# Both heads of a pair in one two-bank score tile, one low-rank add, key copies on ScalarE

## The chip, the cores and the metric

The kernel runs on 1 core of one Trainium2 chip. The metric is device time in microseconds (us) of one execution. A core has TensorE (PE; its weight loads are shown apart as PEld), VectorE (DVE), ScalarE (ACT), GpSimd (POOL) and SyncE (SP), which here only issues DMAs. TensorE writes its results to PSUM, eight banks of 512 float32 columns on 128 partitions.

## What is computed

Two stages. The first is attention in which a query sees the first 8 positions and its own last 96, with a bias that grows with distance; the second is a mixer: a low-rank sum over positions, then a two-layer network, each with a residual.

```python
# q, k, v: (4, 8, 768, 64); n_global 8, n_local 96
scores = q @ k.T / 8
dist   = n_local where is_global & ~is_local, else |i - j|
scores = scores - slope[h] * dist          # slope[h] = 2**-(h + 1) for 8 heads
scores = where(is_global | is_local, scores, -1e9)
a      = softmax(scores)                   # over the keys
x      = (a @ v) with the heads side by side: (4, 768, 512)

h   = x.T @ U @ V                          # U: (768, 32), V: (32, 768)
u   = x + h.T
out = u + relu(u @ w_ch1) @ w_ch2          # w_ch1: (512, 2048), w_ch2: (2048, 512)
```

## The kernel before

The order of instructions on every engine is written out by hand; a framework adds the semaphores. Work goes in pairs of heads: 4 batches of 4 pairs, index `i` from 0 to 15, batch `i // 4`. One pass of the main loop (L774) works on pair `i` and finishes pair `i - 1`.

**Attention of a pair.** The stages are small functions. `cast_qk` turns loaded queries and keys to fp16; `st_T` (pairs 1 to 7) turns them over on TensorE, `turn` (pairs 8 to 15) by DMA. `st_K` (L332) makes `kA`, the keys with the first 8 columns of every block but the first replaced by the global keys, by two VectorE copies. `scores(i, c)` computes chunk `c` of three (512, 512 and 384 columns of a band of 1408) for both heads. The two heads lie in the two halves of the 128 partitions, so their matmuls (L360, L367) have 64 rows each. Each head's scores go to a PSUM tile of one bank, tag `sc`, two buffers.

For batch 0, before the main loop, the bias is added by TensorE (L352) and `st_SE` takes the exponents from PSUM, head by head (L379). Chunks with odd `i + c` use the two `cps` banks instead of `sc`. For the other batches `st_S` lets VectorE add the bias: `s_dve` (L392) computes `score * scale / slope[h] + relcat` into an SBUF tile `sp{hi}`, one step per head and chunk, and `st_E` takes one exponent per head over 1408 columns, scaled by the head's slope (L404). `st_V` multiplies by the values into the bank `ob`, divides (L425, L439), and GpSimd casts the result to `x16` (L440).

**The low-rank sum.** `st_M1` multiplies `x16` by U; for batches 1 to 3 `st_MT` turns the result over with one matmul (L466), of which VectorE copies input and output (`zw` L453, `tmp` L467). `st_M3` multiplies by V in two calls of three matmuls (L503), the first into `sc`, the second into `ob`, one unit of the network later; each call adds its half to `x_sb` (L508). The second also has GpSimd cast `x_sb` to `x16` (L512), and `st_X` issues the DMA that turns that over into `uT`. Batch 0 goes another way (`st_M2`): sums in PSUM, copies to `uT` (L485, L487).

**The network.** Its work is cut into units of about 0.87 us of TensorE, which `fill(n)` puts between the attention steps: *up* units (eight matmuls L609 into a bank of a ring of three, then a relu on ScalarE into `htr`, L614) and *down* units. The first downs are four matmuls of 512 columns (L639). For the last five of the twelve groups of 256 positions (`WG`, L68) the down product is a 2x2 block product with seven instead of eight multiplications: `mk_product` (L659) makes x1, y1, y2, x2, y3, x3, x4, in the last group x1, y1, x2, y2, x3, y3, x4, each followed by an add to `x_sb` (L664). They need sums of the halves of `htr`, s1 to s4, in two parts of 0 to 3 and 4 to 7 of their eight blocks, and sums of weights in `t16`. These VectorE sums are queued as jobs (`queue_sum`); `fill` issues one after each unit, and `need` issues those that a product is about to read. After the main loop the remaining units run alone.

**Around the first main pass.** The bias steps of pair 4, chunk 0, stand by hand between other steps (L763 to L769):

```python
    s_dve(NP, 0, first[0])
    begin_up(0, (0, 1), ps_cps("hps"))
    st_M1(NP - 1)
    s_dve(NP, 1, first[1])
    begin_up(0, (2,))
    begin_up(1, (0, 1, 2), ps_th("hps"))
    st_M2(NP - 1)
```

Of the kernel before, what the change touches and what calls it, by code (L numbers as in the profile page):

```python
# [20 lines left out]
def kernel(  # L21
# [13 lines left out]
    nc = tc.nc  # L35
# [43 lines left out]

    def ps_sc(tag="sc"):  # L80
        return psum.tile([P, 512], FP32, name="sc", tag=tag, bufs=2)

# [82 lines left out]
    warm(8)  # L165
    setup = scp.tile([P, 384], I32, name="setup", tag="ep0")
    reli = setup[:, 0:256]
# [14 lines left out]
    nc.vector.tensor_copy(ident16, ident)  # L182
    relcat = cst.tile([P, 640], FP32, name="relcat")
    rel16 = cst.tile([P, 3, 256], BF16, name="rel16")
# [16 lines left out]
    for vt in vbuf:  # L201
        nc.gpsimd.memset(vt[:, :, :, D:D + 1], 1.0)
    nc.gpsimd.tensor_copy(relcat[:, 0:512].rearrange("p (a c) -> p a c", a=2), rel3[:, 0:2])
    nc.gpsimd.tensor_copy(relcat[:, 512:640], relB[:, 0:P])
    finish_table(
        relcat, relcat[0:NG, 0:512].rearrange("p (a c) -> p a c", a=2)[:, :, P:]
    )

# [134 lines left out]
    def scores(i, c, on_pe):  # L343

        kT, kA, qT = kts[i], kas[i], qts[i]
        c0 = 512 * c
        tot = min(512, W - c0)
        r0 = 256 if c else 0
        scs = [ps_sc("cps" if on_pe and (i + c) % 2 else "sc") for hi in range(2)]
        if on_pe:  # L350
            for hi in range(2):
                nc.tensor.matmul(  # L352
                    scs[hi][:, 0:tot], slI[:, 2 * (i % NP) + hi],
                    rel16.rearrange("p a c -> p (a c)")[:, r0:r0 + tot], start=True, stop=False,
                )
        for kb in (2 * c, 2 * c + 1):
            o = 256 * kb - c0
            for hi in range(2):
                r = slice(hi * D, (hi + 1) * D)
                nc.tensor.matmul(  # L360
                    scs[hi][:, o:o + P], kT[r, kb * P:(kb + 1) * P], qT[r, kb * P:(kb + 1) * P],
                    start=(o == 0 and not on_pe), stop=(o + P == tot),
                )
            if kb < NSB - 1:
                for hi in range(2):
                    r = slice(hi * D, (hi + 1) * D)
                    nc.tensor.matmul(  # L367
                        scs[hi][:, o + P:o + 2 * P], kA[r, kb], qT[r, (kb + 1) * P:(kb + 2) * P],
                        start=False, stop=(o + 2 * P == tot),
                    )  # L370
        return [(sc, c0, tot, r0) for sc in scs]

    def st_SE(i, c):

        if c == 0:
            for hi in range(2):
                eps[i, hi] = scp.tile([P, W], FP16, name=f"ep{hi}", tag=f"ep{hi}")
        for hi, (sc, c0, tot, _) in enumerate(scores(i, c, True)):
# [4 lines left out]
    relfs = (relcat[:, 0:512], relcat[:, 256:512].unsqueeze(1).broadcast_to((P, 2, 256)), relcat[:, 256:640])  # L383

    def s_dve(i, hi, got):
        sc, c0, tot, r0 = got
        if c0 == 0:
            sps[i, hi] = scp.tile([P, W], FP32, name=f"sp{hi}", tag=f"sp{hi}", bufs=1)
        dst, got = sps[i, hi][:, c0:c0 + tot], sc[:, 0:tot]
        if c0 == 512:  # L390
            dst, got = (t.rearrange("p (a c) -> p a c", a=2) for t in (dst, got))
        nc.vector.scalar_tensor_tensor(  # L392
            out=dst, in0=got,
            scalar=qk_scale / slope[2 * (i % NP) + hi], in1=relfs[c0 // 512],
            op0=ALU.mult, op1=ALU.add,
        )

    def st_S(i, c):
        for hi, got in enumerate(scores(i, c, False)):
            s_dve(i, hi, got)  # L400

    def st_E(i, hi):
        ep = scp.tile([P, W], FP16, name=f"ep{hi}", tag=f"ep{hi}")
        nc.scalar.activation(  # L404
            ep, sps.pop((i, hi)), AF.Exp, scale=slope[2 * (i % NP) + hi]
        )
        eps[i, hi] = ep

    def st_V(i, hi):
        b, h = i // NP, 2 * (i % NP) + hi  # L410
        ep, vt, vA = eps.pop((i, hi)), vts[i], vas[i]
        obf = ps_cps("ob") if (i, hi) == (NP - 1, 1) else ps_ob()
# [13 lines left out]
        xo = xs[b][:, :, h * D:(h + 1) * D]  # L426
        x16 = x16s[b][:, i % NP, :, hi * D:(hi + 1) * D]
        rb = rcp.unsqueeze(2).broadcast_to((P, NSB, D))
# [14 lines left out]
    def st_M1(i):  # L443
        b, dc = i // NP, i % NP
        ch = slice(dc * P, (dc + 1) * P)
        if b:
            tps = ps_ob()
            for n in range(NSB):
                nc.tensor.matmul(
                    tps[:, 0:R], x16s[b][:, dc, n], u16[:, n, 0:R],  # L450
                    start=(n == 0), stop=(n == NSB - 1),
                )
            nc.vector.tensor_copy(turn16[i % 2][:, 0:R], tps[:, 0:R])  # L453
            return
        tps = ps_th("tmp_ps")
        for n in range(NSB):
            nc.tensor.matmul(
                tps[:, 0:P], u16[:, n], x16s[b][:, dc, n],
                start=(n == 0), stop=(n == NSB - 1),
            )  # L460
# [8 lines left out]
    def st_M2(i):  # L469
        b, dc = i // NP, i % NP  # L470
        ch = slice(dc * P, (dc + 1) * P)
        for g in range(2):
# [5 lines left out]
            for t in range(NTG):  # L478
                nc.tensor.matmul(
                    ups[:, t * P:(t + 1) * P], x16s[b][:, dc, NTG * g + t], ident16,  # L480
                    start=False, stop=(t == NTG - 1),
                )
# [7 lines left out]
    def st_X(i):  # L490
        b, dc = i // NP, i % NP
        nc.sync.dma_start_transpose(
            uTs[b][:, dc].rearrange("d (n p) -> d n p", n=NSB),
            x16s[b][:, dc].rearrange("p n d -> p (n d)"),
        )

    def st_M3(i, g):
# [13 lines left out]
        if g == 1:  # L511
            nc.gpsimd.tensor_copy(x16s[b][:, dc], xs[b][:, :, ch])  # L512

# [21 lines left out]
    jobs = deque()  # L535
    have = set()

    def queue_sum(name, part, out_, a, b_, op):
        def go():
            nc.vector.tensor_tensor(out_, a, b_, op)  # L540
# [33 lines left out]
    def queue_group(b, g):  # L574
# [9 lines left out]
        def queue_sums(k):  # L584

            h = cell["htr"]
            if k == 0:
                for x in range(1, 5):
                    cell[f"s{x}"] = ffp.tile([P, HJ, P], FP16, name=f"s{x}", tag=f"s{x}", bufs=1)
                cell.update(a11=h[:, 0:HJ, 0:P], a12=h[:, HJ:NJC, 0:P],  # L590
                            a21=h[:, 0:HJ, P:FT], a22=h[:, HJ:NJC, P:FT])
# [99 lines left out]
    def fill(n):  # L691
        for _ in range(n):
            unit()
            if jobs:
                jobs.popleft()()

# [21 lines left out]
    for i in range(NP):  # L718
# [33 lines left out]
        if i == 2:  # L752
            load_w1(1)
        st_SE(i, 2)
        if i >= 2:
# [18 lines left out]
    for i in range(NP, NPAIR + 2):  # L774
# [116 lines left out]
```

## Time and profile before

| | |
|---|---|
| median of 3 runs | 233.54 us (232.63 to 234.28) |
| the profiled execution | 232.94 us |
| its span, first to last instruction | 231.0 us |
| TensorE busy | 223.2 us (97%), 2324 matmuls |
| VectorE busy | 152.7 us (66%), 350 instructions |
| ScalarE busy | 110.9 us (48%), 167 instructions |
| GpSimd busy | 80.5 us (35%), 131 instructions |
| granted TensorE clock, mean | 1.000 |

The profile is one execution. A group of instructions is told by its source line, engine, operation and tile, as output<-input, with the shape as partitions x elements and its count; then follow the busy time, the mean of one in ns, and how long the engine had idled before it and for whom. In a timeline a row gives start, duration, engine, line and operation; a bracket at its end tells an idle time before it and what ended that. Matmuls are pipelined: their starts are measured, their ends are modelled.

### The profile page before, as it was taken

The numbers are of one execution on the slowest core, as the hardware profiler recorded it, in microseconds if no ns is written. First come the engines' busy times: TensorE is split into PE (matmuls) and PEld (weight loads), VectorE is DVE, ScalarE is ACT, GpSimd is POOL, SyncE is SP. The second block draws the span as 40 slices with busy tenths as digits, with TensorE's granted clock in tenths as the row PEclk, the third lists the DMA queues.
The fourth block names the chain that finished last, engine by engine and source line by source line (L and its number), as shares of the span: only waits on it lengthen the run. The fifth ranks groups of instructions, "written<-read, shape, count | busy, mean of one in ns | idle before, by whom it ended". The sixth has DMA issues, their size and how long they took to land.

```text
span 231.0 us, 5678 instructions
## 1 busy us (share of the span) xinstructions
PE 223.2 (97%) x2324; PEld 161.8 (70%) x2324; DVE 152.7 (66%) x350; ACT 110.9 (48%) x167; POOL 80.5 (35%) x131
## 2 busy tenths in 40 slices
PE   7989999999999999999999999999999999999994
PEld 2455678788644457766666656866688888888883
DVE  3697797868677667566656675779895524444452
ACT  6776957685621313827363707473633334333320
POOL 6399728577444243433424051504120100000000
PEclk9999999999999999999999999999999999999999
DMA  6997998999999999897786955633131302011112
GB/s 183 321 280 201 280 203 188 261 259 175 213 210 244 209 315 216 220 182 188 157 226 134 258 140 145 148 100 79 32 81 48 79 3 91 1 48 45 45 48 91
DMA packets 86561, 36.66 MB, mean 159 GB/s; under 512 B 74152, under 2 KB 83592, under 8 KB 86536
## 3 DMA queue, kind: packets, MB, share of 16 engines
q1 hardware_dynamic: 81480, 32.01, 55.1%
q0 software_dynamic: 5056, 4.29, 12.3%
q8 instruction: 18, 0.29, 0.5%
q14 instruction: 7, 0.06, 0.1%
HBM read 27.46 MB, written 6.29 MB: 146 GB/s over the span
## 4 chain that ended last, share of the span: by engine, by line
PE 86%; POOL 3%; DMA 3%; ACT 3%; DVE 2%; issue 1%; SPq 1%; POOLq 0%
PE hps L609 35%; PE cps L639 22%; PE cx L659 8%; PE cy L659 5%; PE sc L360 4%; DMA vst<-in_v_dram 3%; PE ob L420 2%; PE ob L416 2%; PE sc L367 2%; ACT htr L614 1%; ACT ep L404 1%; PE tp L250 1%; PE sc L503 1%; PE ob L503 1%; SPq L105 1%
## 5 line engine op out<-in xcount | busy, mean ns | idle before, releaser
L614 ACT ACTIVATE htr<-hps 128x512 f16<-128x512 f32 x96 | 56.6, 598 | 85.0 <-PE hps L609 82.2
L609 PE MATMUL hps<-uT,w 128*128 128x256 f16 x756 | 96.2, 273 | 0.5 <-DVE uT L485 0.3
L609 PEld LDWEIGHTS <-w 128*128 128x128 f16 x756 | 70.5, 98 | 11.3 <-issue 0.4
L639 PE MATMUL cps<-w,htr 128*128 128x512 f16 x224 | 56.9, 379 | 0.0
L392 DVE SCALAR_TENSOR_TENSOR sp<-sc,relcat 128x512 f32<-128x512 f32 (+1 forms) x72 | 43.3, 641 | 15.5 <-PE sc L360 8.9
L404 ACT ACTIVATE ep<-sp 128x1408 f16<-128x1408 f32 x24 | 32.8, 1374 | 16.3 <-DVE sp L392 16.3
L512 POOL CAST x<-x_sb 128x768 f16<-128x768 f32 x12 | 10.3, 856 | 60.5 <-DVE x_sb L508 60.5
L639 PEld LDWEIGHTS <-htr 128*128 128x128 f16 x224 | 19.1, 97 | 16.6
L440 POOL CAST x<-x_sb 128x384 f16<-128x384 f32 x30 | 15.8, 525 | 26.8 <-DVE x_sb L439 26.7
L360 PEld LDWEIGHTS <-kT 64*128 64x128 f16 x192 | 8.2, 93 | 15.1 <-issue 13.5
L540 DVE TENSOR_TENSOR s<-htr 128x512 f16<-128x512 f16 x20 | 9.3, 464 | 12.7 <-ACT htr L614 12.7
L439 DVE TENSOR_TENSOR x_sb<-ob,rcp 128x384 f32<-128x384 f32 x30 | 16.7, 558 | 1.0
L659 PEld LDWEIGHTS <-s 128*128 128x128 f16 x160 | 15.5, 98 | 1.8
L360 PE MATMUL sc<-qT,kT 64*128 64x128 f16 x192 | 16.7, 221 | 0.0
L420 PE MATMUL ob<-v,ep 128*128 128x65 f16 x192 | 16.2, 193 | 0.0
L420 PEld LDWEIGHTS <-ep 128*128 128x128 f16 x192 | 13.8, 98 | 2.7 <-ACT ep L379 0.3
L664 DVE TENSOR_TENSOR x_sb<-cx,x_sb 128x256 f32<-128x256 f32 x20 | 8.5, 423 | 10.1 <-PE cx L659 10.0
L136 POOL CAST v<-vst 128x768 f16<-128x768 f32 x16 | 13.4, 839 | 4.5 <-DMA vst<-in_v_dram 4.5
L367 PE MATMUL sc<-qT,kA 64*128 64x128 f16 x160 | 14.1, 216 | 0.9 <-DVE kA L286 0.9
L379 ACT ACTIVATE ep<-sc 128x512 f16<-128x512 f32 (+1 forms) x24 | 12.0, 559 | 5.1 <-PE sc L367 4.8
L416 PE MATMUL ob<-vA,ep 128*128 128x65 f16 x160 | 14.3, 194 | 0.2 <-DVE vA L312 0.2
L659 PEld LDWEIGHTS <-htr 128*128 128x128 f16 x120 | 11.7, 98 | 1.3
(102 smaller groups left out, 269.4 us busy)
## 6 DMA issues: line engine op xcount, KB each, us to landing
qst<-in_q_dram SPq DMA_DIRECT2D x16, 384.0 KB, 4.2
kst<-in_k_dram SPq DMA_DIRECT2D x16, 384.0 KB, 4.9
vst<-in_v_dram SPq DMA_DIRECT2D x16, 384.0 KB, 3.4
out_dram<-x_sb SPq DMA_DIRECT2D x23, 256.0 KB, 2.3
w<-in_moe_w_ch_dram POOLq DMA_DIRECT2D x8, 512.0 KB, 8.9
vA<-v SPq DMA_DIRECT2D x8, 152.3 KB, 4.3
out_dram<-x_sb SPq DMA_DIRECT2D x2, 128.0 KB, 1.7
uT<-x SPq DMA_TRANSPOSE x12, 2.8
```

What stands on the lines that cost most here:

```text
L360: nc.tensor.matmul(scs[hi][:, o:o + P], kT[r, kb * P:(kb + 1) * P], qT[r, kb * P:(kb + 1) * P], start=(o == 0 and not on_pe), stop=(o + P ...
L367: nc.tensor.matmul(scs[hi][:, o + P:o + 2 * P], kA[r, kb], qT[r, (kb + 1) * P:(kb + 2) * P], start=False, stop=(o + 2 * P == tot),)
L392: nc.vector.scalar_tensor_tensor(out=dst, in0=got, scalar=qk_scale / slope[2 * (i % NP) + hi], in1=relfs[c0 // 512], op0=ALU.mult, op1=ALU ...
L404: nc.scalar.activation(ep, sps.pop((i, hi)), AF.Exp, scale=slope[2 * (i % NP) + hi])
L416: nc.tensor.matmul(ob[:, qi], ep[:, OF[qi - 1]:OF[qi - 1] + P], vA[:, qi - 1, hi], start=True, stop=False,)
L420: nc.tensor.matmul(ob[:, qi], ep[:, DG[qi]:DG[qi] + P], vt[:, qi, hi], start=(qi == 0), stop=True,)
L439: nc.vector.tensor_tensor(xo, ob[:, :, 0:D], rb, ALU.mult)
L440: nc.gpsimd.tensor_copy(x16, xo)
L609: nc.tensor.matmul(hps[:, k * FT:(k + 1) * FT], w1_16[:, dc, jt * P:(jt + 1) * P], uT[:, dc, ts], start=(dc == 0 and k == 0), stop=(dc == ...
L614: nc.scalar.activation(cell["htr"][:, 2 * jp:2 * jp + 2].rearrange("p j t -> p (j t)"), hps, AF.Relu)
L639: nc.tensor.matmul(cps, htr[:, jc, t * P:(t + 1) * P], w2_16[:, jc], start=(b > 0 and jc == 0), stop=(jc == NJC - 1),)
L659: nc.tensor.matmul(ps, cell[a][:, j], tw[w][:, j], start=(first and j == 0), stop=(done is not None and j == HJ - 1), skip_group_check=True,)
```

## The change

- `ps_sc` gives one tile of two banks, one buffer. `scores` puts head 0 in its first bank and head 1 in its second; where the `cps` banks are used, nothing is changed.
- The bias table has a second half, the first times 0.5 (`st_R`, one multiplication, issued in the third round of batch 0). The slope of head 1 is half that of head 0, so one step with head 0's slope serves both heads: `s_dve` handles both, `sp` and `ep` hold both, and `st_E` scales both exponents by head 0's slope. In batch 0 one exponent step takes both heads of a chunk that lies in `sc`.
- `st_M3` is one call with six matmuls into the two-bank tile and one add of 768 columns; the cast to `x16` follows at the place of the former first call. `st_X` stays where it was.
- `x16` is a tile per pair, three buffers, instead of one per batch, two buffers.
- `st_K` copies the keys on ScalarE, without the 8 global columns; VectorE fills those for all five blocks.
- s3 is written over a quarter of `htr`; `t16` has a buffer of its own instead of one of `x_sb`. Jobs for s1 to s4 may be issued by `fill` only two units later than before.

```diff
-    def ps_sc(tag="sc"):
-        return psum.tile([P, 512], FP32, name="sc", tag=tag, bufs=2)
+    def ps_sc():
+        return psum.tile([P, 2, 512], FP32, name="sc", tag="sc", bufs=1)
...
-        x16s[b] = xp.tile([P, NP, NSB, P], FP16, name="x16", tag="x16")
...
-        nc.vector.tensor_copy(kA.rearrange("d n p -> d (n p)"), kT[:, 0:S - P])
+        nc.scalar.copy(kA[:, :, NG:], kT.rearrange("d (n p) -> d n p", n=NSB)[:, 0:NSB - 1, NG:])
         nc.vector.tensor_copy(
-            kA[:, 1:, 0:NG], kT[:, 0:NG].unsqueeze(1).broadcast_to((P, NSB - 2, NG))
+            kA[:, :, 0:NG], kT[:, 0:NG].unsqueeze(1).broadcast_to((P, NSB - 1, NG))
         )
...
-        scs = [ps_sc("cps" if on_pe and (i + c) % 2 else "sc") for hi in range(2)]
+        both = None if on_pe and (i + c) % 2 else ps_sc()
+        scs = [ps_cps("sc") if both is None else both[:, hi] for hi in range(2)]
...
+        if both is not None:
             nc.scalar.activation(
-                eps[i, hi][:, c0:c0 + tot], sc[:, 0:tot], AF.Exp, scale=qk_scale
+                eps[i][:, :, c0:c0 + tot], both[:, :, 0:tot], AF.Exp, scale=qk_scale
             )
...
+    def st_R():
+        nc.vector.tensor_scalar_mul(relcat2[:, 1], relcat, 0.5)
+
+    relfs = (relcat2[:, :, 0:512], relcat2[:, :, 256:768], relcat2[:, :, 256:640])
...
         nc.vector.scalar_tensor_tensor(
-            out=dst, in0=got,
-            scalar=qk_scale / slope[2 * (i % NP) + hi], in1=relfs[c0 // 512],
+            out=sps[i][:, :, c0:c0 + tot], in0=both[:, :, 0:tot],
+            scalar=qk_scale / slope[2 * (i % NP)], in1=relfs[c0 // 512],
             op0=ALU.mult, op1=ALU.add,
         )
...
-            ep, sps.pop((i, hi)), AF.Exp, scale=slope[2 * (i % NP) + hi]
-        )
+            eps[i][:, hi], sps[i][:, hi], AF.Exp, scale=slope[2 * (i % NP)]
+        )
...
-        ups = ps_ob() if g else ps_sc()
-        for t in range(NTG):
-            n = NTG * g + t
+        ups = ps_sc()
+        for n in range(NSB):
+            g, t = divmod(n, NTG)
             nc.tensor.matmul(
-                ups[:, t * P:(t + 1) * P], v16w[:, n * P:(n + 1) * P], tmps[b][:, ch],
+                ups[:, g, t * P:(t + 1) * P], v16w[:, n * P:(n + 1) * P], tmps[b][:, ch],
                 start=(t == 0), stop=(t == NTG - 1),
             )
-        dst = xs[b][:, NTG * g:NTG * (g + 1), ch]
+        dst = xs[b][:, :, ch].rearrange("p (g t) d -> p g t d", g=2)
         nc.vector.tensor_tensor(
-            dst, ups[:, 0:GT].rearrange("p (t d) -> p t d", t=NTG), dst, ALU.add
-        )
-        if g == 1:
-            nc.gpsimd.tensor_copy(x16s[b][:, dc], xs[b][:, :, ch])
+            dst, ups[:, :, 0:GT].rearrange("p g (t d) -> p g t d", t=NTG), dst, ALU.add
+        )
+        nc.gpsimd.tensor_copy(x16s[i], xs[b][:, :, ch])
...
-    def queue_sum(name, part, out_, a, b_, op):
+    count = [0]
+
+    def queue_sum(name, part, out_, a, b_, op, wait=0):
         def go():
             nc.vector.tensor_tensor(out_, a, b_, op)
             have.add((name, part))
-        jobs.append(go)
+        jobs.append((count[0] + wait, go))
...
-        t = xp.tile([P, 3, HJ, HD], FP16, name="t16", tag="x_sb", bufs=3)
+        t = wbig.tile([P, 3, HJ, HD], FP16, name="t16")
...
-                queue_sum((name, b, g), k, cell[name][:, js], cell[a][:, js], cell[b_][:, js], op)
+                queue_sum((name, b, g), k, cell[name][:, js], cell[a][:, js], cell[b_][:, js], op, wait=2)
...
             unit()
-            if jobs:
-                jobs.popleft()()
+            count[0] += 1
+            if jobs and jobs[0][0] < count[0]:
+                jobs.popleft()[1]()
...
         if i == 2:
             load_w1(1)
+            st_R()
         st_SE(i, 2)
...
     st_M2(NP - 2)
-    s_dve(NP, 0, first[0])
+    s_dve(NP, first)
     begin_up(0, (0, 1), ps_cps("hps"))
     st_M1(NP - 1)
-    s_dve(NP, 1, first[1])
     begin_up(0, (2,))
...
         if i > NP:
-            st_M3(i - 1, 0)
+            st_M3(i - 1)
         if live:
             st_E(i, 1)
         fill(next(units))
         if i > NP:
-            st_M3(i - 1, 1)
             st_X(i - 1)
```

More of the change, by code (lines that the diff above doesn't have):

```diff
@@ L165 @@
     warm(8)
-    setup = scp.tile([P, 384], I32, name="setup", tag="ep0")
+    setup = scp.tile([P, 384], I32, name="setup", tag="ep")
     reli = setup[:, 0:256]
@@ L182 @@
     nc.vector.tensor_copy(ident16, ident)
-    relcat = cst.tile([P, 640], FP32, name="relcat")
+    relcat2 = cst.tile([P, 2, 768], FP32, name="relcat")
+    relcat = relcat2[:, 0]
     rel16 = cst.tile([P, 3, 256], BF16, name="rel16")
@@ L202 @@
         nc.gpsimd.memset(vt[:, :, :, D:D + 1], 1.0)
[L203 to L206, printed above, removed]
-    )
+    relcat3 = relcat.rearrange("p (a c) -> p a c", a=3)
+    nc.gpsimd.tensor_copy(relcat3, rel3)
+    finish_table(relcat, relcat3[0:NG, :, P:])
     def load_uv():
@@ L370, in scores, with s_dve @@
                     )
[L371 removed]
+        return scs, both, c0, tot
     def st_SE(i, c):
         if c == 0:
[L376 to L378 removed]
+            eps[i] = scp.tile([P, 2, W], FP16, name="ep", tag="ep")
+        scs, both, c0, tot = scores(i, c, True)
+        if both is not None:
             nc.scalar.activation(
[L380 removed]
+                eps[i][:, :, c0:c0 + tot], both[:, :, 0:tot], AF.Exp, scale=qk_scale
             )
[L383 to L386 removed]
+            return
+        for hi, sc in enumerate(scs):
+            nc.scalar.activation(
+                eps[i][:, hi, c0:c0 + tot], sc[:, 0:tot], AF.Exp, scale=qk_scale
+            )
+    def st_R():
+        nc.vector.tensor_scalar_mul(relcat2[:, 1], relcat, 0.5)
+    relfs = (relcat2[:, :, 0:512], relcat2[:, :, 256:768], relcat2[:, :, 256:640])
+    def s_dve(i, got):
+        _, both, c0, tot = got
         if c0 == 0:
[L388 to L391, printed above, removed]
+            sps[i] = scp.tile([P, 2, W], FP32, name="sp", tag="sp", bufs=1)
         nc.vector.scalar_tensor_tensor(
[L393 to L394 removed]
+            out=sps[i][:, :, c0:c0 + tot], in0=both[:, :, 0:tot],
+            scalar=qk_scale / slope[2 * (i % NP)], in1=relfs[c0 // 512],
             op0=ALU.mult, op1=ALU.add,
@@ L398, in st_S @@
     def st_S(i, c):
-        for hi, got in enumerate(scores(i, c, False)):
-            s_dve(i, hi, got)
+        s_dve(i, scores(i, c, False))
     def st_E(i, hi):
-        ep = scp.tile([P, W], FP16, name=f"ep{hi}", tag=f"ep{hi}")
+        if hi == 0:
+            eps[i] = scp.tile([P, 2, W], FP16, name="ep", tag="ep")
         nc.scalar.activation(
-            ep, sps.pop((i, hi)), AF.Exp, scale=slope[2 * (i % NP) + hi]
+            eps[i][:, hi], sps[i][:, hi], AF.Exp, scale=slope[2 * (i % NP)]
         )
-        eps[i, hi] = ep
     def st_V(i, hi):
         b, h = i // NP, 2 * (i % NP) + hi
-        ep, vt, vA = eps.pop((i, hi)), vts[i], vas[i]
+        ep, vt, vA = eps[i][:, hi], vts[i], vas[i]
+        if hi == 0:
+            x16s[i] = xp.tile([P, NSB, P], FP16, name="x16", tag="x16", bufs=3)
         obf = ps_cps("ob") if (i, hi) == (NP - 1, 1) else ps_ob()
```

18 lines of the change are left out of this document (9 added, 9 removed).

## The prediction

> **What bounds the kernel.** I read the page's busy times first, then busy time by stage, then the groups by shape, and last the timelines of four places. The profiled execution took 232.94 us; its span is 231.0, so 1.94 lie around it, which the change does not touch. The median of the runs is 233.54, 0.60 above the profiled one.
>
> Busy time by stage (us of PE, PEld, DVE, ACT, POOL in each stretch; the columns after them are clock, DMA share, GB/s):
>
> ```profile
> 0.00:35.00 35.00, 30.86 (x381) 19.36 (x382) 25.82 (x67) 24.29 (x48) 23.57 (x48) 1.00 0.99 246
> 35.00:180.00 145.00, 144.64 (x1511) 99.94 (x1509) 104.80 (x227) 70.83 (x94) 56.12 (x83) 1.00 0.79 175
> 180.00:231.00 51.00, 47.68 (x437) 42.48 (x435) 22.11 (x57) 15.82 (x27) 0.83 (x1) 1.00 0.15 51
> ```
>
> From 35 to 180 us TensorE is busy for 144.64 of 145.00, at granted clock 1.00, and VectorE has 40 us to spare. The change keeps every matmul (2324 before and after), so nothing it saves on VectorE or ScalarE there can shorten the run by more than the few waits of TensorE. Measured as starts that come later than the column counts of the matmuls explain, the waits of over 70 ns after 34 us, row-group switches left out, are six: 0.25, 0.16, 0.21, 0.08, 0.17 and 0.39, together 1.26 us. What the change can add, it adds where TensorE is waiting on others or would soon be: the first 35 us and the last 10.
>
> **The parts.** The prices come from these groups (busy us, mean ns | idle before):
>
> ```profile
> L392 DVE SCALAR_TENSOR_TENSOR sp<-sc,relcat 128x512 f32<-128x512 f32 x48 | 31.0, 685 | 6.6 <-PE sc L367 5.7 <-ACT ep L404 0.4
> L392 DVE SCALAR_TENSOR_TENSOR sp<-sc,relcat 128x384 f32<-128x384 f32 x24 | 12.3, 552 | 8.9 <-PE sc L360 8.9
> L272 ACT COPY qT<-tp 128x768 f16<-128x768 f16 x7 | 5.6, 804 | 0.3 <-PE tp L250 0.2
> L122 DVE CAST k<-kst 128x768 f16<-128x768 f32 x2 | 1.1, 546 | 0.0
> ```
>
> *Bias step.* 685 and 552 ns give 1.04 ns a column and 152 ns fixed, so one step over 2x512 is 1.22 us and over 2x384 0.95. Back to back, two old steps took 1.28 and 1.02: VectorE gains about 0.06 x 36, 2 us in all, where it has 40 spare. New wait: one step must wait for both exponents of the pair before, which read the same tile. Head 1's exponent ended after head 0's step had started three times (41.20, 51.18 and 61.30 against 40.12, 50.71 and 60.83), so the merged step ends about 0.5 later there. Behind it are the reciprocal, the division and the key turn on VectorE; TensorE comes back for the score tile at 43.20, 53.32 and 62.96, 0.4 to 0.9 after the new ends (42.45, 52.44, 62.55). Price 0. If that cover is gone, up to 0.5 each.
>
> *The first merged step* is different: it used to be split around a small copy.
>
> ```profile
> 29.85 0.68 DVE L392 SCALAR_TENSOR_TENSOR sp<-sc,relcat 128x512 f32<-128x512 f32 x1
> 30.45 0.28 DVE L461 CAST tmp<-tmp_ps 128x128 f16<-128x128 f32 x1
> ...
> 31.01 0.33 PE L474 MATMUL ups<-v16w,tmp 128*128 128x384 f16 x1
> ```
>
> The copy moves from 30.45 to 29.85 + 1.14 = 30.99 and ends at 31.27; the matmul that reads it starts at 31.01 now and at 31.30 then, and TensorE already waits at 32.15 for what follows it. **+0.3**, between 0.2 and 0.5.
>
> *Half-slope table.* One new 128x768 f32 multiplication on VectorE at about 22.2 us, ahead of the uT copies. Between 20.4 and 27.1 VectorE idles 0.14 us before 23.27 and little else, and at 27.13 TensorE waits for its last copy, so nearly all of it shows. Alone it is near the L122 cast, 0.55 (a 1x rate, as 953 ns in L273, would make it 0.95). But GpSimd is casting then, and a VectorE copy that meets GpSimd can be held:
>
> ```profile
> 22.01 0.89 POOL L122 CAST q<-qst 128x768 f16<-128x768 f32 x1
> 22.85 0.82 POOL L122 CAST k<-kst 128x768 f16<-128x768 f32 x1
> ...
> 37.61 2.40 DVE L312 COPY vA<-v 8x520 f16<-8x520 f16 x1 [0.47 <-POOL vA L299]
> ```
>
> The 8x520 copy takes 0.27 alone; here it sat until GpSimd's two casts ended at 39.86. In six other meetings (0.46 to 0.84 us) it got in after one GpSimd instruction. Three values: held by nothing, VectorE is 0.31 late at 23.27 and 0.2 at 27.13; held by the q cast to 22.90, the multiplication ends near 23.4, the k cast after it near 24.2 (TensorE's k transposes need it at 23.73), and 27.13 becomes 27.9, **+0.8**; held by both casts to 23.67, VectorE runs 1.85 late at 23.27 and 27.13 becomes 28.5, +1.4. I take 0.8, the commoner row.
> The Trainium skill (SBUF — State Buffer, Who interferes with whom) says that VectorE's two-port modes and GpSimd share one port pair, that whoever issues first holds it for the whole instruction and the other blocks fully; the 2.40 us row agrees. By that rule alone the multiplication waits for the q cast only, and the sum is the middle one.
>
> *Exponents of batch 0.* Six pairs become one step of 2x512 or 2x384: 595 and 488 ns give 0.84 a column, so 1.02 against 1.09 for a pair. The score tile of chunk (2,0) is freed at 15.87 instead of 15.36 and its matmul waits 0.17, but that chunk waits at 16.71 for key copies anyway. 0.
>
> *Key copies.* VectorE loses 319 ns, ScalarE gains 600 columns (from 475 ns at 384 and 804 at 768, about 0.66) eight times. ScalarE idles over half the span; behind the copy stand a relu and an exponent, and three hps banks cover about 3 us. The keys are used 2.5 us later or more. 0; if the banks ran out, up to 0.66 each.
> The Trainium skill (ScalarE: Activation LUTs, Rules for kernel authors) puts simple elementwise work on VectorE, not ScalarE; 319 ns against an estimated 660 agrees. By it the move loses 0.34 x 8 = 2.7 us of engine time, none of it on the path.
>
> *Low-rank sum, x16, t16.* Two adds of 556 ns become one of about 0.95; six matmuls stand together and need both score banks, free since the third bias step, one unit and more before. The cast and so the transpose start about 0.9 sooner; SP's place of the transpose is unchanged, loads and stores behind it wait less. The only tight one is issued at 180.86 with a median landing of 2.8, 183.66, for matmuls at 183.85: none waited. 0, or a wait avoided. The own t16 buffer ends no wait that the trace shows.
>
> *Deferred sums.* They now enter VectorE's queue two units later, s3 in place. Gain: at 176.46 TensorE lost 0.39 because a sum waiting for a relu stood ahead of the small zw copy; there, and at 172.08 and 171.04 (0.25), the queue is now clear: **-0.5**, between -0.1 and -1.0. Loss: in the last group no up units stand between the products, and "two units later" is behind the add of y1:
>
> ```profile
> 222.23 0.42 DVE L540 TENSOR_TENSOR s<-htr 128x512 f16<-128x512 f16 x1 [1.95 <-ACT htr L614]
> 222.27 1.04 PE L659 MATMUL cy<-w,htr 128*128 128x256 f16 x8
> ...
> 222.91 0.41 DVE L540 TENSOR_TENSOR s<-s,htr 128x512 f16<-128x512 f16 x1
> 223.15 1.04 PE L659 MATMUL cx<-t,s 128*128 128x256 f16 x8
> 223.35 0.42 DVE L664 TENSOR_TENSOR x_sb<-cy,x_sb 128x256 f32<-128x256 f32 x1
> ```
>
> New order on VectorE: add x1, add y1, s1, s2, add x2, s4, add y2, s3. The add of y1 cannot start before 223.35; at 0.34 a step s1 starts 223.69, s2 224.03 and ends 224.45. Product x2 needs s2's second half at its fifth matmul, due 223.59: it waits to 224.51, +0.92. Then y2 ends at 226.0, its add runs from 226.03, s3 from 226.37 to 226.78; x3 needs it at 226.26, +0.58. **+1.5** on the chain that ends last, with no slack but the final store's 2.85 us, which moves along. Bounds 1.2 and 1.8.
>
> Sum: 0.3 + 0.8 - 0.5 + 1.5 = **+2.1**: 235.0 for an execution like the profiled one, 235.6 on the median.
>
> **Rivals.** About 1% (2.3 us) is what a measurement here tells from no change.
> 1. *The multiplication stays shut out through both casts* (the 37.61 row, same two casts): +1.4 instead of 0.8, sum +2.7, 236.2, slower by over 1%. It decides if the multiplication ends after 24.0. Against it: six meetings that ended after one instruction. 0.22.
> 2. *The multiplication meets no cast*, because it slips in ahead of q: sum +1.5, 235.0. For: the copy before it did so at 22.06. 0.18.
> 3. *The merged bias step becomes what TensorE waits for* at chunk 1 of every pair: it decides once the step ends after the margins above; three early pairs late by 0.5 give +1.5 more, 237.1. Against: only 0.4 us of waiting on exponents in the whole trace. 0.07.
> 4. *The deferral pays and the end does not stall* (the half sums s1 and s2 get in ahead of the add of y1, or x2 runs on its first half long enough): 0.3 + 0.8 - 1.3 + 0.1, about -0.1, 233.4. Against: the order of a queue is fixed when the program is built. 0.08. Faster by over 1% needs more than all 1.26 us of waits.
>
> My case has 0.45. Its own range is 234.8 to 236.3; with rivals 1, 2 and the run-to-run spread of 0.7 the range is 233.9 to 237.0. Slower by over 1%: 0.38 of my case (it lies 0.2 below the line), most of rival 1 and 3, together 0.41; faster 0.03; the rest 0.56.
>
> **What would show it.** After: a multiplication row near 22.2, its length and the next POOL cast's start (step 1 if it ends at 23.4); TensorE's copy wait near 27.13 moved to 27.9; the tmp copy behind a 1.22 us step; no wait before the small transposing matmul near 176; and two gaps of 0.9 and 0.6 in the last six products. Wrong if those products run at 0.87 each, or if waits on merged steps show between 35 and 180.

## The result and the profile after

The changed kernel's median is 236.78 us (235.91 to 237.11, 4 runs), against 233.91 us for the kernel before on the same chip (232.63 to 238.06, 4 runs): a ratio of 1.0128, 95% interval 1.0084 to 1.0173. The change made the kernel slower by 1.3%, about 3.0 us. The forecast was 235.6 us in a range of 233.9 to 237.0: the range held, the point was 1.2 too low. Medians, here and below, are over all runs, while ratios leave out runs in the chip's slower state (here the one of 238.06), and since both mended kernels below were profiled in such a run, only their waits are read and not their spans.

The profiled execution of the changed kernel took 237.11 us, its span is 235.3 (before 232.94 and 231.0). First the busy times, then busy time by stage (us of PE, PEld, DVE, ACT, POOL in each stretch, then clock, DMA share and GB/s), over stretches that end at about the same work as those of before:

```profile
PE 224.8 (96%) x2324; PEld 161.4 (69%) x2324; DVE 147.8 (63%) x295; ACT 114.8 (49%) x169; POOL 81.4 (35%) x130
```

```profile
0.00:36.30 36.30, 31.43 (x380) 19.17 (x381) 25.77 (x66) 24.28 (x42) 24.08 (x47) 1.00 1.00 241
36.30:182.70 146.40, 145.29 (x1511) 99.92 (x1509) 98.90 (x171) 74.73 (x102) 57.34 (x83) 1.00 0.80 173
182.70:235.30 52.60, 48.03 (x437) 42.32 (x435) 23.11 (x60) 15.83 (x27) 0.00 (x0) 1.00 0.15 50
```

VectorE has 55 instructions fewer and 4.9 us less work than before. The first stretch grew by 1.3, the middle by 1.4, the last by 1.6. VectorE's saving lies in the middle (98.90 us instead of 104.80), and TensorE got through that stretch no sooner, but later. The waits of TensorE say for whom it waited (us in total, times, longest):

```profile
PE cx L667 <- DVE s L548: 0.9, 1, 0.9
...
PE sc L360 <- DVE x_sb L515: 0.5, 2, 0.2
...
PE cx L667 <- DVE htr L548: 0.4, 1, 0.4
...
PE ob L427 <- DVE x_sb L446: 0.2, 1, 0.2
```

None of the four stands in the list of before. The two `cx` rows are the last products, as forecast. The `sc` row is new: scores that wait for the low-rank add. The `ob` row, an output product that waits for VectorE's division (`x_sb` L446), is new too.

Since the matmuls are the same 2324 in both programs, the same matmul can be found in both traces, and its start after minus its start before can be followed through the run. Apart from places where the program's order differs, it is flat for long stretches and rises in steps. A second profile of the same program (the first run below) has the steps at the same places:

| at (us, after) | step | in the repeat | what TensorE waits for | forecast |
|---|---|---|---|---|
| 0 to 20 | +0.54 | +0.41 | first key and value loads | none |
| 24.7 | +0.45 | +0.45 | k cast behind the half-slope multiplication | +0.8 |
| 32.3 | +0.31 | +0.32 | small copy behind the first merged step | +0.3 |
| 48.5 | +0.29 | +0.30 | x16 cast, late by a wait for exponents | 0 |
| 52.0, 62.5 | +0.62 | +0.63 | low-rank add that holds both score banks | 0 |
| 66.9, 70.2 | +0.33 | 0 | not the same in both profiles | none |
| 91.8 | +0.24 | +0.13 | turn of x by DMA | 0 |
| 163.9, 168.4 | +0.56 | +0.56 | sums of weights and halves before the division and the zw copy | 0 |
| 171 to 180 | -0.65 | -0.64 | old waits gone | -0.5 |
| 227.3, 229.7 | +1.63 | +1.63 | sums behind adds in the last group | +1.5 |

The rows add up to 4.3 us, the difference of the two spans. Without the loads' luck in the first row and at 67 to 70, 3.5 us are left (3.4 in the repeat). The wait for a turn at 91.8 is not shown to be the change's either: against the kernel before it has another size in each of the other traces, 0.10 to 1.81 us. Without it 3.2 us are left in both profiles, and these belong to the change.

### The profile page after: what moved, and what is told of

Same layout as the page of the kernel before. It is cut to its first block, busy times and chain, and to the rows that moved or that the text cites. A ratio compares the mean times of both kernels' runs of the same rounds, so it can differ in the third digit from the quotient of the medians.

```text
span 235.3 us, 5605 instructions
## 1 busy us (share of the span) xinstructions
PE 224.8 (96%) x2324; PEld 161.4 (69%) x2324; DVE 147.8 (63%) x295; ACT 114.8 (49%) x169; POOL 81.4 (35%) x130
## 4 chain that ended last, share of the span: by engine, by line
PE 74%; DVE 9%; DMA 7%; POOL 4%; issue 3%; ACT 2%; SPq 1%; DVEq 0%; POOLq 0%
PE hps L617 30%; PE cps L647 19%; PE cx L667 7%; PE cy L667 6%; DMA kst<-in_k_dram 5%; PE sc L360 3%; DVE sp L398 2%; PE ob L427 2%; PE sc L510 2%; PE ob L423 1%; DMA uT<-x 1%; ACT ep L410 1%; PE sc L367 1%; DVE t L548 1%; DVE x_sb L515 1%
## 5 line engine op out<-in xcount | busy, mean ns | idle before, releaser
L398 DVE SCALAR_TENSOR_TENSOR sp<-sc,relcat 128x1024 f32<-128x1024 f32 (+1 forms) x36 | 40.8, 1133 | 20.4 <-PE sc L360 9.3
L647 PEld LDWEIGHTS <-htr 128*128 128x128 f16 x224 | 19.4, 97 | 17.2
L446 DVE TENSOR_TENSOR x_sb<-ob,rcp 128x384 f32<-128x384 f32 x30 | 16.7, 557 | 1.0
L667 PEld LDWEIGHTS <-htr 128*128 128x128 f16 x160 | 15.5, 98 | 2.5 <-DVE htr L548 0.7
L515 DVE TENSOR_TENSOR x_sb<-sc,x_sb 128x768 f32<-128x768 f32 x12 | 11.5, 955 | 7.7 <-PE sc L510 7.7
L667 PEld LDWEIGHTS <-s 128*128 128x128 f16 x120 | 11.6, 98 | 2.5 <-DVE s L548 1.1
L672 DVE TENSOR_TENSOR x_sb<-cy,x_sb 128x256 f32<-128x256 f32 x15 | 6.4, 425 | 10.2 <-PE cy L667 10.0
```

Source lines behind the costliest of these rows:

```text
L398: nc.vector.scalar_tensor_tensor(out=sps[i][:, :, c0:c0 + tot], in0=both[:, :, 0:tot], scalar=qk_scale / slope[2 * (i % NP)], in1=relfs[c0 ...
L446: nc.vector.tensor_tensor(xo, ob[:, :, 0:D], rb, ALU.mult)
L647: nc.tensor.matmul(cps, htr[:, jc, t * P:(t + 1) * P], w2_16[:, jc], start=(b > 0 and jc == 0), stop=(jc == NJC - 1),)
L667: nc.tensor.matmul(ps, cell[a][:, j], tw[w][:, j], start=(first and j == 0), stop=(done is not None and j == HJ - 1), skip_group_check=True,)
```

## The experiments

All kernels below are edits of the changed kernel, except the last, which edits the kernel before. Ratios are to the kernel before on the same chip. "Step" is a step of that table, read from the trace of the experiment.

**The same again.** No edit.

> The changed kernel again, nothing edited. Theory A (the change's cost is a sum of local waits that its own instructions cause, about 3.1 us of the 4.3 by which the profiled spans differ; 0.54 us of the 4.3 is the luck of when the first key and value loads land) expects +2.9 to +3.2 us against the kernel before (ratio 1.012 to 1.014), the same waits at the same places in the profile (23.7, 32.3, 48.5, 52.0, 62.5, the last 10 us), and a first key cast that doesn't always start 0.4 us late. Rival B (the later start belongs to the change, through the larger table or the setup) expects the key cast late by 0.3 to 0.4 us here too, and +3.4 us or more.

Measured: 237.07 us, ratio 1.0151 (1.0101 to 1.0201). The steps stand in the table. By this run alone rival B would stand: 1.0151 is +3.5 us, and VectorE's first key cast is late here too (9.54 us, 9.66 in the first profile, 9.28 in the kernel before). But in the two-add kernel below, with the same first 20 us, it starts at 8.81. The offset at 20 us, +0.41 here, lies between -0.69 and +1.08 in the other edits of the changed kernel, of which all but three have the same first 20 us, and their mean is about zero. So the start is chance.

**The last group's sums at once.**

```diff
-  queue_sum(..., cell[b_][:, js], op, wait=2)
+  queue_sum(..., cell[b_][:, js], op, wait=0 if last else 2)
```

> The last group's half sums are queued at once, all other groups' still two units later. Theory A (the last six products wait because the sums stand behind the add of y1: 1.04 + 0.57 us in the profile) expects -1.6 us against the changed kernel, ratio to the kernel before 1.006, products 0.87 us apart without a gap. The rival (the end is bound by the final add and store, and the sums only use up slack) expects less than -0.5 us, ratio above 1.010.

Measured: 235.05 us, ratio 1.0053 (1.0015 to 1.0090). The last products in the timeline, first of the changed kernel (start, duration, engine, line, operation), then of this one:

```profile
225.86 0.60 PE L667 MATMUL cx<-t,s 128*128 128x256 f16 x4
227.33 0.61 PE L667 MATMUL cx<-t,s 128*128 128x256 f16 x4 [0.87 <-DVE s L548]
...
228.65 0.60 PE L667 MATMUL cx<-w,htr 128*128 128x256 f16 x4
229.66 0.61 PE L667 MATMUL cx<-w,htr 128*128 128x256 f16 x4 [0.41 <-DVE htr L548]
```

```profile
226.34 1.04 PE L667 MATMUL cx<-t,s 128*128 128x256 f16 x8
227.21 1.04 PE L667 MATMUL cy<-t,s 128*128 128x256 f16 x8
228.08 1.04 PE L667 MATMUL cx<-w,htr 128*128 128x256 f16 x8
228.96 1.04 PE L667 MATMUL cy<-w,s 128*128 128x256 f16 x8
```

x2 and x3 were cut in two after four matmuls; now each product follows the last by 0.87. Theory A holds, also in the time: by the ratios 1.8 to 2.3 us less than the two measurements of the changed kernel.

**Every sum at once.** `wait=0` for all groups.

> Every half sum is queued at once; the other parts of the change stay. Theory A (the deferral costs 1.6 us in the last group and saves 0.65 us before it, at 171 to 176 us) expects -0.95 us against the changed kernel, ratio to the kernel before 1.0085 to 1.009, the waits of 0.25 to 0.4 us before the small transposing matmuls near 171 to 176 back, and 0.6 us more than with the last group alone undone. The rival (the deferral saves nothing, since other sums of the weights stand there anyway) expects the same time as with the last group alone undone, ratio 1.006.

Measured: 235.00 us, ratio 1.0053 (1.0022 to 1.0083). By the time this is the rival's case: theory A's 1.0085 to 1.009 lies just outside the interval, and the run above has the same ratio. The trace shows why the two are close: at 180 the wait before the small transposing matmul is back,

```profile
179.96 0.23 PE L473 MATMUL ob<-ident,zw 128*128 128x128 f16 x1 [0.23 <-DVE zw L460]
```

and the step of -0.40 there is gone, and with it the +0.15 that the deferred sums cost at 168. The -0.25 at 171 to 172 stays. So of the 0.65 the deferral gives 0.40, and it takes 0.15, a net 0.25 that the time can't tell from nothing; the other 0.25 has another cause, which is neither the deferral nor (see the last run) the weights' own buffer. Writing s3 in place is the part that both of these kernels have, but it wasn't tried alone.

**The low-rank sum as two adds.**

```diff
-    def st_M3(i):                       # six matmuls, one add, cast of x
+    def st_M3(i, g):                    # as before, in two calls
+        ups = ps_ob() if g else ps_sc()[:, 0]
...
```

> The low-rank sum as two adds again: the first half's matmuls in one bank of the score tile, the second half's a unit later in the output bank; x16 and the turn of x follow the second add as in the kernel before. Theory A (in batch 1 the merged add holds both score banks with one unit between it and the next pair's scores, 0.31 us at 52.0 and 62.5) expects those two waits gone, -0.6 us against the changed kernel, ratio 1.010. The rival (the merged tile alone is at fault, and any writer of it a unit earlier is waited for as long; or x being turned a unit later costs it back) expects no change, ratio 1.0125 or more.

Measured: 235.27 us, ratio 1.0048 (1.0006 to 1.0091): more came back than theory A's ratio of 1.010. TensorE and VectorE where the next pair's scores follow, first of the kernel before, then of the changed kernel, then of this one:

```profile
48.83 0.33 PE L503 MATMUL sc<-tmp,v16w 128*128 128x128 f16 x3
50.13 0.23 PE L360 MATMUL sc<-qT,kT 64*128 64x128 f16 x2
```

```profile
49.26 0.56 DVE L508 TENSOR_TENSOR x_sb<-sc,x_sb 128x384 f32<-128x384 f32 x1 [0.82 <-PE sc L503]
```

```profile
50.44 0.50 PE L510 MATMUL sc<-tmp,v16w 128*128 128x128 f16 x6
50.77 1.04 PE L617 MATMUL hps<-uT,w 128*128 128x256 f16 x8
52.05 0.23 PE L360 MATMUL sc<-qT,kT 64*128 64x128 f16 x2 [0.24 <-DVE x_sb L515]
```

```profile
51.05 0.96 DVE L515 TENSOR_TENSOR x_sb<-sc,x_sb 128x768 f32<-128x768 f32 x1 [0.99 <-PE sc L510]
```

```profile
49.22 0.33 PE L510 MATMUL sc<-tmp,v16w 128*128 128x128 f16 x3
49.38 1.04 PE L618 MATMUL hps<-uT,w 128*128 128x256 f16 x8
50.26 0.33 PE L510 MATMUL ob<-tmp,v16w 128*128 128x128 f16 x3
50.52 0.23 PE L360 MATMUL sc<-qT,kT 64*128 64x128 f16 x2
```

```profile
49.66 0.56 DVE L515 TENSOR_TENSOR x_sb<-sc,x_sb 128x384 f32<-128x384 f32 x1 [0.82 <-PE sc L510]
```

The merged add ends at 52.01 and the scores start at 52.05: one unit of 0.87, begun at 50.77, stands between the six matmuls and the scores, while the add ends 1.24 after that. With two adds only the first, of 0.56, must be through with the tile, and it is 0.3 before the scores start. Both steps are gone, and the +0.41 at 163.9 and the +0.15 behind it as well, which the expectation had not named. The trace accounts for 1.2 us of the gain (from 20 us on, 2.14 behind the kernel before instead of the repeat's 3.38); the time shows 1.9 to 2.4 by the ratios, and the rest is within the intervals.

Why 163.9? In the changed kernel (VectorE, then GpSimd, then TensorE):

```profile
157.30 0.96 DVE L515 TENSOR_TENSOR x_sb<-sc,x_sb 128x768 f32<-128x768 f32 x1 [0.31 <-PE sc L510]
158.17 1.91 DVE L548 TENSOR_TENSOR t<-w,t 128x1024 f16<-128x1024 f16 x2
160.01 1.21 DVE L398 SCALAR_TENSOR_TENSOR sp<-sc,relcat 128x1024 f32<-128x1024 f32 x1
```

```profile
158.32 1.22 POOL L518 CAST x<-x_sb 128x768 f16<-128x768 f32 x1 [5.00 <-DVE x_sb L515]
```

```profile
163.86 0.19 PE L427 MATMUL ob<-v,ep 128*128 128x65 f16 x1 [0.25 <-DVE x_sb L446]
```

Two sums of weights, back to back 1.28 us elsewhere (161.74), take 1.91 here. The first is as long as ever (158.17 to 158.85); GpSimd's cast of x, whose row begins during it, ends at 159.54, and the second sum (158.77 to 160.08, 1.31 instead of 0.68) ends 0.54 after the cast. Everything behind it on VectorE is late by 0.6, and the output product waits. In the kernel before, the bias step behind the sums starts here:

```profile
156.60 1.28 DVE L392 SCALAR_TENSOR_TENSOR sp<-sc,relcat 128x512 f32<-128x512 f32 x2
```

In the changed kernel it starts at 160.01, 3.41 later, where TensorE is 2.80 behind. Without the 0.63 that the second sum lost, VectorE would be no later than TensorE, so the merged add's own length doesn't explain the wait. With two adds, the sum before the cast (156.36 to 157.04) has the port first, the cast takes 1.15 from 156.58, and the next on VectorE is a bias step, which runs its usual 1.22. The rows fit the rule of the Trainium skill (SBUF — State Buffer, Who interferes with whom) that a VectorE instruction with two inputs in SBUF, as these sums are, contends with a GpSimd instruction that reads SBUF, and that the one of the two that is shut out waits for the other's whole instruction.

**The cast of x a unit later, the merged add kept.**

```diff
 def st_X(i):
     ...
+    nc.gpsimd.tensor_copy(x16s[i], xs[b][:, :, dc * P:(dc + 1) * P])
...
 def st_M3(i):
     ...
-    nc.gpsimd.tensor_copy(x16s[i], xs[b][:, :, ch])
```

> The merged low-rank add stays, but GpSimd's cast of x behind it, and so the turn of x, comes a unit later, as in the kernel before. Theory A (near 158 us that cast, a unit sooner, keeps the port while a sum of the weights on VectorE wants it: 1.31 us instead of 0.68, and the output product at 163.9 waits 0.41) expects that wait gone and the sum at 0.68, while the waits at 52.0 and 62.5 stay: -0.4 to -0.55 us against the changed kernel. The rival (the 0.41 comes from the merged add's own place on VectorE) expects the wait to stay.

Measured: 236.86 us, ratio 1.0127 (1.0087 to 1.0167). The wait stays, by the letter of the expectation the rival's case. But the trace shows that the edit moved nothing:

```profile
159.05 1.91 DVE L547 TENSOR_TENSOR t<-w,t 128x1024 f16<-128x1024 f16 x2
```

```profile
159.20 1.22 POOL L499 CAST x<-x_sb 128x768 f16<-128x768 f32 x1 [5.00 <-DVE x_sb L516]
```

GpSimd had idled for 5.00 us and nothing else stood in its queue, so the cast started 0.06 us after the add's end at 159.14, as in the changed kernel. That the cast is what holds the sum rests on the rows and on the two-add kernel, not on this run.

**The half-slope table on ScalarE, early.**

```diff
     st_T(0)
+    st_R()
     warm(2)
...
-        nc.vector.tensor_scalar_mul(relcat2[:, 1], relcat, 0.5)
+        nc.scalar.mul(relcat2[:, 1], relcat, 0.5)
...
-            st_R()
```

> The half-slope table is made on ScalarE near 7 us, where ScalarE waits for the first scores, instead of on VectorE at 22.7. Theory A (the multiplication takes the port ahead of GpSimd's cast of q, which takes 1.36 us instead of 0.89, so the cast of k and TensorE's turn of it come 0.45 us late) expects a q cast of 0.84 to 0.89 us, no step of TensorE at 23.7, -0.45 us against the changed kernel. The rival (VectorE itself is late by the multiplication and the casts only look long) expects the step to stay at 0.2 or more. A step in the first 10 us would mean that ScalarE's copies were pushed back.

Measured: 236.47 us, ratio 1.0135 (1.0069 to 1.0201); the time doesn't show 0.45 us (0.2%). The trace does. In the changed kernel:

```profile
22.19 0.55 DVE L311 COPY vA<-v 8x520 f16<-8x520 f16 x1
22.66 0.54 DVE L390 TENSOR_SCALAR relcat<-relcat 128x768 f32<-128x768 f32 x1
```

```profile
22.53 1.36 POOL L123 CAST q<-qst 128x768 f16<-128x768 f32 x1
23.84 0.82 POOL L123 CAST k<-kst 128x768 f16<-128x768 f32 x1
```

```profile
24.72 0.45 PE L249 MATMUL tp<-ident,k 128*128 128x128 f16 x5 [0.26 <-POOL k L123]
```

and with the table on ScalarE:

```profile
21.53 0.89 POOL L123 CAST q<-qst 128x768 f16<-128x768 f32 x1
22.37 0.82 POOL L123 CAST k<-kst 128x768 f16<-128x768 f32 x1
```

The multiplication was not held at all: its 0.54 is what the prediction took for it alone. It was GpSimd that waited, with 1.36 instead of 0.89, and that is the 0.45 by which TensorE's k transposes came late. The cast's row begins 0.13 before the multiplication's, but VectorE was still in its copy of vA then, and the multiplication followed that copy without a gap. Without the multiplication there, the step at 24.7 is gone. On ScalarE the table takes 0.84 at 7.03, in an idle stretch.

**The first bias step in two again.** One step for head 0, the small copy, one for head 1, as in the kernel before.

> The first bias step of batch 1 is two steps again, one for each head, with the small copy between them as in the kernel before. Theory A (the copy waits for the longer step: 0.32 us before the low-rank matmul at 32.3) expects that step of 0.3 us gone, -0.3 us against the changed kernel, nothing else moved. The rival (the copy waits for its matmuls, which come late anyway) expects no change.

Measured: 236.63 us, ratio 1.0135 (1.0079 to 1.0192); the step at 32.3 is gone from the trace:

```profile
29.84 0.68 DVE L407 SCALAR_TENSOR_TENSOR sp<-sc,relcat 128x512 f32<-128x512 f32 x1
30.43 0.28 DVE L477 CAST tmp<-tmp_ps 128x128 f16<-128x128 f32 x1
```

The copy starts 0.59 after the step ahead of it; in the changed kernel it started 1.13 after it (30.85 and 31.98). Again 0.3 us is less than the time can tell.

**A second buffer for the summed scores.** `sp` with two buffers; `t16` back in the ring of `x_sb`, for room.

> The summed scores get a second buffer, so that a merged bias step need not wait for the exponents of the pair before; to make room, the weights' sums take their buffer from the ring of x, as in the kernel before. Theory A (the merged step waits for both exponents, which once, in pair 5, reaches TensorE: 0.30 us before the low-rank product at 48.5, while the other pairs' waits lie beside other work) expects the wait at 48.5 gone, those at 52.0 and 62.5 unchanged, -0.3 us against the changed kernel. The rival (rival 3 of the prediction: the exponents' waits are what makes the scores late in every early pair) expects 52.0 and 62.5 gone too, -0.9 us. If the buffer of the weights' sums matters, a new wait shows near 150 to 160.

Measured: 236.26 us, ratio 1.0113 (1.0051 to 1.0175). The step at 48.5 is gone, those at 52.0 and 62.5 stay, and no step is new between 93 and 165, so the weights' own buffer is worth nothing here. In the changed kernel the chain begins at the merged step, which waits for both exponents:

```profile
42.55 1.23 DVE L398 SCALAR_TENSOR_TENSOR sp<-sc,relcat 128x1024 f32<-128x1024 f32 x1 [1.23 <-ACT ep L410]
```

Behind it come, in this order, the division, the key turn, GpSimd's copies of keys and values, and its cast of x16 to 48.42, for which TensorE waits at 48.48. With two buffers the same cast ends at 47.05, 0.56 before the product that needs it starts. This profile also waits 1.45 us for weights at 67.5, of which more below.

**Key copies back on VectorE.** `st_K` as in the kernel before.

> The key copies of the later pairs back on VectorE, all else as changed. Theory A (the copies lie beside other work on either engine, priced 0) expects no step of TensorE gone or new, the changed kernel's time, ratio 1.0125 to 1.015. The rival (ScalarE's relus and exponents stand behind the copies) expects steps gone between 110 and 180 us and 0.3 us or more less.

Measured: 237.62 us, ratio 1.0153 (1.0115 to 1.0192), the same as the repeat's 1.0151, and every step of the repeat from 24.7 on is in the trace, the one at 91.8 in another size. Against the expectation a step of 0.69 at 74 is new: the scores wait 0.62 for the low-rank add, which stands on VectorE behind the rest of the key copies, and these wait for a turn of the keys by DMA:

```profile
72.10 0.33 DVE L334 COPY kA<-kT 128x640 f16<-128x640 f16 x1 [1.39 <-DMA kT<-k]
```

That is not the move's doing: the kernel with every sum at once, which copies the keys on ScalarE, has the same step (0.71), with a key copy of 8 columns a block held by the same turn. The move is worth nothing, as priced.

**Four parts mended.** The last group's sums at once, two low-rank adds, the table on ScalarE, the first step in two.

> Four parts undone or moved at once: the last group's sums at once, the low-rank sum as two adds, the half-slope table on ScalarE at 7 us, the first bias step in two. Theory A (the cost is the sum of local waits, each with its own cause) expects 1.62 + 1.2 + 0.45 + 0.32 = 3.6 us less than the changed kernel between 20 us and the end, that is 0.2 to 0.4 us faster than the kernel before (ratio 0.998 to 1.000). The rival (the waits share slack: where one is taken away the next takes its place) expects 2.5 us or less to come back, ratio 1.004 or more.

Measured: 233.33 us, ratio 1.0005 (0.9959 to 1.0051). By the ratios 2.9 to 3.4 us come back, of the 3.6 expected; none of the steps at 24.7, 32.3, 52.0, 62.5, 163.9 and 227 is in the trace. Theory A holds: the waits add up and did not replace each other. That it is faster than the kernel before is not shown.

**All mended, and two buffers for the sums.**

> All four parts mended as in the run before, and the summed scores with a second buffer (the weights' sums back in the ring of x for room). Theory A (local waits that add up) expects the wait of 0.30 us before 48.5 gone too, no step of TensorE left between 20 us and 165 but the one near 89 whose size differs from run to run, -0.65 us in the last quarter: 0.3 to 0.7 us faster than the kernel before, ratio 0.997 to 0.999. The rival (the kernel before is bound by the same matmuls, so nothing can be had) expects 1.000 or more.

Measured: 233.59 us, the fastest run 231.84, ratio 0.9959 (0.9909 to 1.0010). The step at 48.5 is gone too and the -0.65 is there, but the interval holds 1. It has the lowest ratio of these kernels, but that it is faster than the kernel before, or than the four parts alone, is not shown.

**The deferral alone, in the kernel before.** Jobs two units later except in the last group, s3 in place.

> The kernel before with the deferral alone: half sums two units later except in the last group, s3 in place. Theory A (it takes away the waits of 0.25 and 0.39 us near 171 and 176) expects -0.4 to -0.65 us against the kernel before, ratio 0.997 to 0.998. The rival (the gain near 171 comes from another part of the change, such as the weights' sums in a buffer of their own) expects -0.25 us or less.

Measured: 237.41 us (236.55 to 238.57), ratio 1.0156 (1.0114 to 1.0197), against both theories. The profile has the forecast gain: from 168 to 180 the offset falls by 0.65, from +4.05 to +3.40. The loss came long before:

```profile
PE cps L642 <- DMA w<-in_moe_w_ch_dram: 2.3, 2, 1.5
...
PE hps L612 <- DMA uT<-x: 0.7, 1, 0.7
```

TensorE waits at 64.48 and 67.37 for quarters of the second weight matrix, and at 92.9 for a turn of x. The order of the instructions doesn't explain those waits: up to VectorE's sum at 160 us every engine has the same instructions in the same order as in the kernel before. The loads landed late. Loads issued from 44 to 70 us, with the median from issue to landing in us at the end, first of the kernel before, then of this one:

```profile
w<-in_moe_w_ch_dram POOLq DMA_DIRECT2D x4, 512.0 KB, 8.9
kst<-in_k_dram SPq DMA_DIRECT2D x2, 384.0 KB, 8.5
```

```profile
w<-in_moe_w_ch_dram POOLq DMA_DIRECT2D x4, 512.0 KB, 11.3
kst<-in_k_dram SPq DMA_DIRECT2D x2, 384.0 KB, 12.8
```

All six runs of this program lay at 236.55 or more, while the kernel before ran at 232.69 to 235.78 beside it, so it is hardly chance from run to run alone. What in the program or its place in memory does it stays open; no run tells it apart. The profiles of the two-buffer kernel and of both mended kernels show the same wait for weights (1.4, 3.0 and 3.2 us), with these quarters landing after 11.3 to 12.5 us; the other profiles don't, and there they land after 8.6 to 11.0. Those three profiled executions took 237.89, 237.91 and 237.69 us, where others of the same kernels took as little as 235.59, 232.82 and 231.84, so in them the wait probably doesn't come with every execution.

## Why the prediction was right, and where it was not

The forecast was "+2.1", the trace shows 3.2 of waits that repeat, the two measurements 3.0 and 3.5 (1.3 and 1.5% of 234). The side held, and so did the range; the sum was short by 1.1. That the range held is in part luck: it reached up to 237.0 for rival 1 and the spread of the runs, while terms priced at 0 added 1.5 and the half-slope table, priced too high, hid 0.35 of that. The repeat's median, 237.07, lies just above it. Step by step:

- *What bounds the kernel* was right: VectorE does 5.9 us less in the middle stretch, and only the waits of 0.65 near its end went away.
- *First merged step*, +0.3: measured 0.31, and gone when the step is split.
- *Half-slope table*, +0.8: the place was right, the mechanism wrong. "Held by the q cast to 22.90" did not happen; the multiplication got in ahead of the cast, as in rival 2. But rival 2's price, 0.2, counted only VectorE's own delay. The other side was left out: the cast was held, and that cost 0.45.
- *Deferred sums in the last group*, +1.5: measured 1.63. The first wait was 1.04 instead of 0.92, since s2, which reads s1, follows it by 0.45 (226.40 and 226.85) and not by 0.34.
- *Deferred sums before it*, -0.5: measured -0.65, of which 0.40 is the deferral's by the run without it. It also cost 0.15 at 168, which was not in the sum.
- *Low-rank sum*, 0: **this step failed**, a wait that the sum put at nothing. "Six matmuls [...] need both score banks, free since the third bias step" asks only who used the tile earlier. It did not ask who needs it next: the scores, one unit later, now wait for the whole add of 0.96, where they had needed only a half of 0.56, made a unit earlier. That cost 0.31 in each of two pairs, 0.62 in all, and it was gone with two adds.
- *The transpose "about 0.9 sooner"*, priced as nothing or a gain: the cast of x that comes with it meets the sums of weights at 158 and costs 0.41 at 163.9. The meeting is shown by the rows; the run meant to move the cast alone did not move it. The turn itself was issued no sooner (88.47 against 84.42, where TensorE is 2.6 behind), after other DMAs of SP, and the wait of 0.24 for it at 91.8 is seen in all sizes from 0.10 to 1.81 us, in the kernels without a merged add too.
- *Merged bias step*, 0, "if that cover is gone, up to 0.5 each": gone once, in pair 5, for 0.29, and not at the score tile but at the end of the chain behind it. Rival 3 as a general case falls: with the exponents' wait taken away nothing else moved.
- *Exponents, key copies, buffer of t16*, 0 each: no step anywhere; the last two shown by a run each.

## What to carry to other kernels

When two steps are merged over one larger PSUM tile, price the next user of every bank, not only the step that got cheaper: the tile comes free when the longest reader ends. A delay counted in slots of other work needs an exception where that work runs out, as in a last group. Where two engines hold each other up, price the loser's delay whichever of them loses.

## What was not expected of the hardware

A cast on GpSimd that is held up by VectorE is shown as running: 22.53 to 23.89 is one row of 1.36 us, 0.47 longer than the 0.89 without the multiplication. Which of the two goes first can't be read from where the rows begin. At 22.53 the cast's row begins before the multiplication's, and the multiplication goes first; at 158.32 the cast's row begins before the second sum's, and the cast goes first.

Two programs with the same instructions on every engine up to 160 us differed by 1.6% in time (1.0114 to 1.0197), and the profile of the slower one has 2.3 us of waits for weights that landed after 11.3 us instead of 8.9. So a ratio near 1 between two programs of this kernel can't by itself be put down to an edit. Steps at the same matmul that repeat in two traces can; apart from waits for loads and turns by DMA they agree to some 0.02 us here.
